# Layer-norm roots of one token block moved from ScalarE to GpSimd, an earlier table load and one matmul tile moved ahead, in a fused attention and gMLP kernel

## The chip, the cores and the metric

The kernel runs on one core of a Trainium2 chip. The metric is the device time of one execution in microseconds (us). Times inside an execution are microseconds from the start of the profiled span. The engines are named as in the profile: PE is TensorE (PEld its weight loads), DVE is VectorE, ACT is ScalarE, POOL is GpSimd, SP is SyncE, whose queue issues nearly all DMAs.

## The reference

The input x has 2048 tokens of 512 channels. It is layer-normalized without weights, and two branches are added to it.

```
xn  = layernorm(x)                        # (x - mean) / sqrt(var + 1e-5)
# branch A: 32 heads of 16, each token attends to 8 tokens: t, t-2, ..., t-14
q, k, v = split(xn @ wqkv)
o   = softmax(mask(q . k[t - 2w]) / 4) applied to v[t - 2w]
A   = o @ wo
# branch B: gMLP, hidden size 688
z   = gelu_tanh(xn @ w_in);  z1, z2 = halves of z
z2  = layernorm(z2)
g   = w_sp @ z2 + b_sp                    # over the 2048 tokens
B   = (z1 * g) @ w_out
out = x + A + B
```

## The kernel before

The 2048 tokens are 16 tiles of 128. Tile i = 4*tb + j belongs to block j (0 to 3); a block so holds the four tiles (tb = 0 to 3) that lie 512 tokens apart. The program is one fixed order of instructions for each engine, written out by hand (no scheduler moves anything): first straight code for the four x blocks, then a string `ORDER` of tokens, each of which issues one step.

**The straight code.** Per tile: `ln_stats` (two DVE instructions, mean and variance into `mv`), `ln_root` (one ACT instruction, `rstd = 1/sqrt(var + eps)`), `ln_apply` (one DVE instruction, x normalized in place), and a transpose into `xnT`, by PE and a copy for the first tiles and by `tr_dma`, a DMA transpose from SP's queue, for the last two tiles of block 1 (`i1`) and all of blocks 2 and 3 (`i2`, `i3`). Between them PE runs q and k of blocks 0 and 1: `qk_part` issues matmuls for two of the four channel chunks of q or k, into a tile `pq` of the main PSUM pool `ps_mm` (three buffers) or `pa3` of the auxiliary pool `ps_aux` (two buffers of one bank), and `qk_copy` is the ACT copy to SBUF. A buffer can be written again only when its copy is done. In block 1 the last of these steps, (1, 3) for tiles 2 and 3, takes a fourth `pq` tile, and the one `ln_root` for all four tiles of block 3 stands on ACT just before its copy; the four applies and DMA transposes of block 3 follow.

**ORDER.** The tokens that matter here: `zJ.T` is a z2 tile, eight matmuls of 344 columns into a `ps_mm` buffer for tile T of block J (L257); `zgJ.T` its gelu on ACT (L275), which frees the buffer; `zsJ.T` a sum of squares on ACT (L281); `qJ.M` and `qcJ.M` are eight matmuls of 512 columns of q or k of block J, which need all four tiles of the block (L315), and their ACT copy (L331); `pG.C` is a DVE product of q and shifted k (L355); `aG` and `bG` are DVE sums over its chunks (L364, L367); `LG` the logits matmuls of group G (L375), which read what `bG` leaves; `X` are the z1 tiles; `wN` loads a tile of w_sp through SP's queue. The order starts

```
z1.3 z2.0 p1.1 z2.2 zg1.3 p0.1 zg2.0 q2.2 zg2.2 p0.3 zs2.2 q2.3 p1.2 qc2.2 p1.3 q2.1 qc2.3 p1.0 z1.0 p0.2
```

Gelu needs another function table on ACT than the roots; the load (L275, ACT_TABLE_LOAD) stands in front of the first gelu, zg1.3.

GpSimd builds a few constants at the start, casts the bias `b` to `b_col` once its DMA has landed (L684), and clears a halo (L697).

Of the kernel before, what the change touches and what calls it, by code (L numbers as in the profile page):

```python
# [8 lines left out]
F32 = mybir.dt.float32  # L9
ACT = mybir.ActivationFunctionType  # L10
ALU = mybir.AluOpType
# [3 lines left out]
P = 128  # L15
# [23 lines left out]
ORD = [1, 2, 3, 0]  # L39
CHUNKS = (1, 1, 1, 1, 1, 1, 1, 1)  # L40
ORDER = """
z1.3 z2.0 p1.1 z2.2 zg1.3 p0.1 zg2.0 q2.2 zg2.2 p0.3 zs2.2 q2.3 p1.2 qc2.2 p1.3 q2.1 qc2.3 p1.0 z1.0 p0.2
qc2.1 w3 z2.1 p0.0 zg1.0 zs1.0 q2.0 p2.2 zg2.1 a1 z2.3 qc2.0 w2 z1.2 zg2.3 p2.3 halo zs2.0 z3.0 p2.0 zg1.2
z1.1 w0 zg3.0 b1 z0.1 zg1.1 p2.1 zs2.3 X0 a0 zg0.1 z3.2 Xg0 zs1.1 z3.3 a2 zg3.2 z3.1 zs1.2 zg3.3 z0.2 b0 zg3.1
X4 b2 zg0.2 zs3.3 L0 L1 Xg4 q3.1 p3.2 zs3.1 p3.0 Lc0 q3.0 Lc1 p3.1 qc3.1 q3.2 p3.3 qc3.0 zs0.1 a3 z0.3 qc3.2
q3.3 zg0.3 p4.1 zs1.3 p4.0 z0.0 qc3.3 X1 p4.2 zg0.0 zs0.3 X2 p4.3 Xg1 X5 st.0 zs2.1 st.1 a4 Xg2 L2 V6 zs0.2
zs3.2 b3 Xg5 V2 b4 Vc6 zs0.0 p5.3 L3 V5 zs3.0 p5.2 Vc2 V1 st.2 p5.1 Vc5 p5.0 V0 st.3 a5 w4 Lc2 Vc1 V4 st.4 Vc0
w1 N1.1 V3 N2.0 Vc4 N1.0 b5 Lc3 V7 N0.0 Vc3 M0.0 N1.2 M0.1 L5 N0.2 L4 Vc7 N3.3 X6 N0.1 M0.2 N0.3 late X3 N3.1
N1.3 N2.1 G0.0 N2.2 Xg6 N2.3 N3.2 N3.0 G0.1 p7.1 G0.2 M0.3 G0.3 p7.2 G4 p6.0 Gi0 w6 Lc4 p6.3 Xg3 p6.2 E0 p7.3
G3 p6.1 U0 S0.0 p7.0 a6 w9 G1 Gi3 Gi4 S0.1 b6 a7 G2 Gi1 w7 U1 S0.2 b7 S0.3 w5 S0.4 Lc5 R0 L6 L7 G6 Lc6 A0 Gi2  # L50
Lc7 U2 U4 mask T4 U3 M1.0 A1 T2 G7 A2 Gi6 w8 A3 wo1.2 A4 T0 A5 X7 M1.1 Gi7 A6 wo1.3 xr0 G5 A7 Xg7 A8 w10 M1.2
# [13 lines left out]
def slot_w(s):  # L65
    return 4 * (s // 4) + 3 - s % 4
# [3 lines left out]
def kernel(  # L70
# [14 lines left out]
    A = nc.scalar  # L85
    G = nc.gpsimd
# [7 lines left out]
    sb = ctx.enter_context(tc.tile_pool(name="sb", bufs=1))  # L94
    work = ctx.enter_context(tc.tile_pool(name="work", bufs=3))
    ps_mm = ctx.enter_context(tc.tile_pool(name="ps_mm", bufs=3, space=PSUM))
    ps_aux = ctx.enter_context(tc.tile_pool(name="ps_aux", bufs=2, space=PSUM))
# [41 lines left out]
    z2 = sb.tile([P, NT, FH], BF16, name="z2")  # L139
# [11 lines left out]
    mv = sb.tile([P, NT, 2], F32, name="mv")  # L151
    rstd = sb.tile([P, NT], F32, name="rstd")
# [4 lines left out]
    zvar = sb.tile([P, NT], F32, name="zvar")  # L157
    zrstd = sb.tile([P, NT], F32, name="zrstd")
    eps_t = sb.tile([P, 1], F32, name="eps_t")


    k_casts = [[] for _ in range(4)]
# [30 lines left out]
                    base=0, pattern=[[-1, P]], channel_multiplier=1)  # L193
    V.memset(ks[:, :, 0:HALO], 0.0)
    V.memset(z1u[:, 0:NZ1 - 1, FH:FPAD], 0.0)
    G.memset(rsel[:], 1.0)
    G.affine_select(out=rsel[:], in_=rsel[:], compare_op=ALU.is_ge, fill=0.0,
                    base=0, pattern=[[-4, 32]], channel_multiplier=1)
# [8 lines left out]
    def ln_stats(i, parts=1):  # L207
        j, tb = i % 4, i // 4
        w = D // parts
        for h in range(parts):  # L210
            V.bn_stats(stats[:, i, 6 * h:6 * h + 6], xall[:, j, tb, w * h:w * h + w])  # L211
        ln_agg(i, parts)
# [4 lines left out]
    def ln_agg(i, parts=1):  # L217
        V.bn_aggr(mv[:, i, :], stats[:, i, 0:6 * parts])  # L218

    def ln_root(sl):  # L220
        A.activation(rstd[:, sl], mv[:, sl, 1], ACT.Abs_reciprocal_sqrt, bias=eps_t[:])

    def ln_apply(i):
        j, tb = i % 4, i // 4
        V.tensor_scalar(xall[:, j, tb, :], xall[:, j, tb, :], mv[:, i, 0:1], rstd[:, i:i + 1],  # L225
                        ALU.subtract, ALU.mult)
# [22 lines left out]
    def tr_dma(i):  # L249
        j, tb = i % 4, i // 4  # L250
        SP.dma_start_transpose(xnT[:, :, i * P:(i + 1) * P], xall[:, j, tb, :])
# [10 lines left out]
    table = [None]  # L262
# [20 lines left out]
    def z2_var():  # L283
        return [lambda: V.tensor_scalar(zmean[:], zsum[:], 1.0 / FH, None, ALU.mult),
                lambda: V.tensor_tensor(zm2[:], zmean[:], zmean[:], ALU.mult),
                lambda: V.scalar_tensor_tensor(zvar[:], zsq[:], 1.0 / FH, zm2[:], ALU.mult, ALU.subtract)]
# [22 lines left out]
    def qk_part(pq, j, m, b0, b1, ccs=(0, 1), p0=None, kcs=range(C)):  # L309
        sd, c0 = m // 2, 2 * (m % 2)  # L310
        p0 = b0 if p0 is None else p0
        xv = xnT[:].rearrange("p k (b j t) -> p k b j t", b=TB, j=4)
        for cc in ccs:
            for kc in kcs:
                PE.matmul(pq[:, cc, p0 * P:(p0 + b1 - b0) * P], wqk[:, sd, kc, c0 + cc:D:C],  # L315
                          xv[:, kc, b0:b1, j, :], start=(kc == 0), stop=(kc == C - 1))
# [7 lines left out]
    def qk_copy(pq, j, m, b0=0, b1=TB, p0=None):  # L324
        sd, c0 = m // 2, 2 * (m % 2)
        p0 = b0 if p0 is None else p0
        if sd == 0:
            dst = qs[:, j, c0:c0 + 2, b0 * P:b1 * P].rearrange("p c (b t) -> p c b t", b=b1 - b0)
        else:
            dst = ks[:, c0:c0 + 2, HALO:HALO + S].rearrange("p c (b j t) -> p c b j t", b=TB, j=4)[:, :, b0:b1, j, :]  # L330
        cast = A.copy(dst, pq[:, :, p0 * P:(p0 + b1 - b0) * P].rearrange("p c (b t) -> p c b t", b=b1 - b0))  # L331
        if sd == 1:
            for i in k_reads[j]:
                tc.declare_no_dep(cast.ins, i, reason="other token columns of the same rows")
            k_casts[j].append(cast.ins)

    def qk_tile():
        return ps_mm.tile([P, 2, TBS], F32, name="pq", tag="mm")
# [8 lines left out]
    def prod_c(g, c):  # L347

        o, h = g // 2, g % 2
        j = ORD[o]  # L350
        q3 = qs[:, j, c, :].rearrange("p (b t) -> p b t", b=TB)
        off = HALO - DIL * slot_w(4 * h)
        k3 = ks[:, c, off:off + S].rearrange("p (b j t) -> p b j t", b=TB, j=4)[:, :, j, :]
        k4 = bass.AP(k3.tensor, k3.offset, [list(x) for x in k3.ap[0:2]] + [[DIL, 4], list(k3.ap[2])])
        prod = V.tensor_tensor(pr[g % 3][:, c].rearrange("p w b t -> p b w t"),  # L355
                        q3.unsqueeze(2).broadcast_to([P, TB, 4, P]), k4, ALU.mult)
        for jj in range(4):
            if jj not in (j, (j - 1) % 4):
                for i in k_casts[jj]:
                    tc.declare_no_dep(prod.ins, i, reason="other token columns of the same rows")  # L360
                k_reads[jj].append(prod.ins)
# [213 lines left out]
    def blk(j):  # L575
        return [4 * tb + j for tb in range(TB)]
# [4 lines left out]
    def blk_cols(j):  # L581
        return slice(j, NT, 4)
# [7 lines left out]
    i2, i3 = blk(2), blk(3)  # L590
    warm_up(10)
    for n in range(2):
        ln_stats(t0[n], 2)
        ln_root(col(t0[n]))
# [7 lines left out]
    pqs = [qk_tile() for _ in range(3)]  # L602
    ln_stats(t0[2])
    ln_root(col(t0[2]))
    tr_copy(t0[1], pts[1], 2, 4)
    q_tile(0, (0, 1))
# [6 lines left out]
    pt2 = tr2(t0[2])  # L613
    q_tile(1, (2, 3))
    ln_root(col(t0[3]))
    tr_copy2(t0[2], pt2)
    ln_apply(t0[3])
# [38 lines left out]
        ln_stats(i2[n])  # L656
    ln_root(slice(2, 7, 4))
    ln_root(slice(10, 15, 4))
    for i in i2:
        ln_apply(i)  # L660
        tr_dma(i)
    for n in range(4):
        ln_stats(i3[n])
    pqs = [qk_tile() for _ in range(3)]
    for c in range(3):
        qk_part(pqs[c], 1, c, 0, 2)
    pa3 = ps_aux.tile([P, 2, 2 * P], F32, name="pa3", tag="aux")
    qk_part(pa3, 1, 3, 0, 2)
    qk_copy(pa3, 1, 3, 0, 2)
    for c in range(3):  # L670
        qk_part(pqs[c], 1, c, 2, 4)
        qk_copy(pqs[c], 1, c)
    pqs[0] = qk_tile()
    qk_part(pqs[0], 1, 3, 2, 4)
    ln_root(blk_cols(3))
    qk_copy(pqs[0], 1, 3, 2, 4)
    for i in i3:
        ln_apply(i)
        tr_dma(i)
    SP.dma_start(r_w[:, 4096:6144].rearrange("p (k f) -> p k f", k=C),  # L680
                 A_wqkv[:, 2 * D:3 * D].rearrange("(k p) f -> p k f", p=P))
    SP.dma_start(w_z1[:], B_w_in[:, 0:FH].rearrange("(k p) f -> p k f", p=P))
# [17 lines left out]
    st = z2_var() + [z2_log, z2_exp]  # L700
# [8 lines left out]
    for tok in ORDER.split():  # L709
        name = tok.rstrip("0123456789.")  # L710
# [31 lines left out]
```

## Time and profile before

| | |
|---|---|
| median of 4 runs | 202.19 us (202.16 to 202.43) |
| profiled execution | 202.3 us, span 200.6 us |
| PE busy | 196.1 us, 98% of the span |
| DVE busy | 184.6 us, 92% |
| ACT busy | 104.0 us, 52% |
| POOL busy | 17.8 us, 9% |
| PE clock granted | 1.00 |

A line of a timeline or group gives, in this order, the start, the length, the engine, the line of the kernel, the operation, output and inputs by their names in the program, the shapes and the count; in square brackets stands how long the engine had been idle before, and what ended that. Instructions of one engine overlap a little (a DVE instruction's successor starts some 0.08 us before its end), and matmuls overlap a lot, so pitches are taken from starts.

### The profile page before, as it was taken

The numbers are of one execution on the slowest core, as the hardware profiler recorded it, in microseconds if no ns is written. First come the engines' busy times: TensorE is split into PE (matmuls) and PEld (weight loads), VectorE is DVE, ScalarE is ACT, GpSimd is POOL, SyncE is SP. The second block draws the span as 40 slices with busy tenths as digits, with TensorE's granted clock in tenths as the row PEclk, the third lists the DMA queues.
The fourth block names the chain that finished last, engine by engine and source line by source line (L and its number), as shares of the span: only waits on it lengthen the run. The fifth ranks groups of instructions, "written<-read, shape, count | busy, mean of one in ns | idle before, by whom it ended". The sixth has DMA issues, their size and how long they took to land.

```text
span 200.6 us, 4090 instructions
## 1 busy us (share of the span) xinstructions
PE 196.1 (98%) x1687; PEld 124.5 (62%) x1691; DVE 184.6 (92%) x249; ACT 104.0 (52%) x176; POOL 17.8 (9%) x14
## 2 busy tenths in 40 slices
PE   7999999999999999999999999999999999999994
PEld 2869745665566666666656666666544646664562
DVE  5689999999989999999979999999999999999624
ACT  3586997899899986363431523808402230331400
POOL 3000000699500000000000000000000000000000
PEclk9999999999999999999999999999999999999999
DMA  5976547960000095534377998199930296219863
GB/s 163 264 240 155 108 82 229 239 120 3 0 0 3 3 165 88 161 82 105 49 164 157 243 227 182 33 231 168 209 80 0 76 215 165 72 34 124 215 209 105
DMA packets 66562, 25.91 MB, mean 129 GB/s; under 512 B 56496, under 2 KB 66288, under 8 KB 66288
## 3 DMA queue, kind: packets, MB, share of 16 engines
q1 hardware_dynamic: 65824, 25.18, 56.7%
q10 hardware_dynamic: 720, 0.48, 0.8%
q8 instruction: 13, 0.21, 0.5%
q14 instruction: 5, 0.04, 0.1%
HBM read 10.13 MB, written 2.10 MB: 61 GB/s over the span
## 4 chain that ended last, share of the span: by engine, by line
PE 90%; DVE 5%; ACT 3%; issue 1%
PE pg L464 37%; PE pz L257 17%; PE pq L315 7%; PE pv L425 7%; PE po L517 6%; PE po L547 6%; DVE stats L211 3%; PE pwm L586 2%; PE pa L547 2%; PE pq L321 1%; ACT r_qk L331 1%; PE pl L375 1%; DVE r_x L225 1%; DVE mv L218 1%; PE po L526 1%; PE pb L517 1%
## 5 line engine op out<-in xcount | busy, mean ns | idle before, releaser
L464 PE MATMUL pg<-z,r_qk 128*128 128x344 bf16 x448 | 66.8, 309 | 0.0
L464 PEld LDWEIGHTS <-r_qk 128*128 128x128 bf16 x448 | 43.8, 98 | 22.0 <-issue 0.4
L439 DVE TENSOR_TENSOR r_pr<-r_x,r_w 128x2048 bf16<-128x2048 bf16 x32 | 38.4, 1219 | 1.3 <-PE pl L375 1.0
L257 PE MATMUL pz<-w_z,xnT 128*128 128x344 bf16 x256 | 39.3, 309 | 0.0
L443 DVE TENSOR_TENSOR r_pr<-r_pr 128x2048 bf16<-128x2048 bf16 x28 | 33.8, 1217 | 0.4
L257 PEld LDWEIGHTS <-xnT 128*128 128x128 bf16 x256 | 25.0, 98 | 13.2 <-issue 0.4
L470 ACT ACTIVATE gs<-pg,b_col 128x688 bf16<-128x688 f32 x16 | 13.2, 833 | 35.4 <-PE pg L464 26.4
L355 DVE TENSOR_TENSOR r_pr<-r_qk 128x2048 bf16<-128x2048 bf16 x24 | 27.8, 1217 | 0.5 <-ACT r_qk L331 0.5
L315 PE MATMUL pq<-xnT,r_w 128*128 128x512 bf16 (+1 forms) x136 | 24.7, 335 | 0.2 <-ACT z L275 0.2
L315 PEld LDWEIGHTS <-r_w 128*128 128x128 bf16 x144 | 15.8, 114 | 7.9 <-issue 0.8
L684 POOL CAST b_col<-b 128x16 f32<-128x16 bf16 x1 | 15.7, 15738 | 34.2 <-DMA b<-in_B_b_sp_dram 34.2
L530 ACT CAST r_qk<-po 128x512 bf16<-128x512 f32 x10 | 5.5, 588 | 22.7 <-PE po L547 22.7
L331 ACT CAST r_qk<-pq 128x1024 bf16<-128x1024 f32 (+1 forms) x16 | 15.4, 984 | 2.5 <-PE pq L315 2.3
L306 ACT ACTIVATE r_uz<-pz 128x688 bf16<-128x688 f32 x16 | 11.7, 740 | 6.6 <-PE pz L257 6.5
L517 PE MATMUL po<-r_lg,r_pr 32*128 32x512 bf16 x192 | 14.5, 375 | 0.0
L425 PE MATMUL pv<-xnT,r_w 128*32 128x512 bf16 x256 | 14.2, 379 | 0.0
L547 PEld LDWEIGHTS <-r_uz 128*128 128x128 bf16 x85 | 8.0, 98 | 9.5 <-issue 1.1
L364 DVE TENSOR_TENSOR r_pr<-r_pr 128x4096 bf16<-128x4096 bf16 x6 | 13.7, 2284 | 0.0
L547 PE MATMUL po<-r_w,r_uz 128*128 128x512 bf16 x56 | 12.7, 379 | 0.5 <-issue 0.5
L281 ACT ACTIVATE junk<-z 128x688 bf16<-128x688 bf16 x16 | 12.4, 774 | 0.1
L275 ACT ACTIVATE z<-pz 128x688 bf16<-128x688 f32 x16 | 11.8, 740 | 1.2 <-PE pz L257 1.2
L425 PEld LDWEIGHTS <-r_w 128*32 128x32 bf16 x256 | 9.5, 138 | 4.2
(85 smaller groups left out, 196.1 us busy)
## 6 DMA issues: line engine op xcount, KB each, us to landing
r_lg<-in_A_wo_dram SPq DMA_DIRECT2D x8, 256.0 KB, 4.0
r_x<-in_A_x_dram SPq DMA_DIRECT2D x12, 128.0 KB, 2.9
out_dram<-r_qk SPq DMA_DIRECT2D x12, 128.0 KB, 2.1
r_w<-in_A_wqkv_dram SPq DMA_DIRECT2D x8, 128.0 KB, 3.4
r_qk<-in_A_x_dram SPq DMA_DIRECT2D x8, 128.0 KB, 2.2
w_z<-in_B_w_in_dram SPq DMA_DIRECT2D x4, 172.0 KB, 4.2
w_z<-in_B_w_in_dram SPq DMA_DIRECT2D x1, 688.0 KB, 5.4
r_w<-in_B_w_out_dram SPq DMA_DIRECT2D x1, 640.0 KB, 6.5
```

What stands on the lines that cost most here:

```text
L257: PE.matmul(pz[:, hh, 0:FHALF], xnT[:, kc, i * P:(i + 1) * P], wz[:, kc, hh * FHALF:(hh + 1) * FHALF], start=(kc == 0), stop=(kc == C - 1))
L315: PE.matmul(pq[:, cc, p0 * P:(p0 + b1 - b0) * P], wqk[:, sd, kc, c0 + cc:D:C], xv[:, kc, b0:b1, j, :], start=(kc == 0), stop=(kc == C - 1))
L331: cast = A.copy(dst, pq[:, :, p0 * P:(p0 + b1 - b0) * P].rearrange("p c (b t) -> p c b t", b=b1 - b0))
L355: prod = V.tensor_tensor(pr[g % 3][:, c].rearrange("p w b t -> p b w t"), q3.unsqueeze(2).broadcast_to([P, TB, 4, P]), k4, ALU.mult)
L364: V.tensor_tensor(pr[g % 3][:, 0:2], pr[g % 3][:, 0:2], pr[g % 3][:, 2:4], ALU.add)
L425: PE.matmul(pv[32 * tb:32 * tb + 32, dd, :], wv[:, kc, 2 * d2 + dd, :], xnT[:, kc, tb * TBS:(tb + 1) * TBS], start=(kc == 0), stop=(kc == ...
L439: V.tensor_tensor(pw_t[n], vp[:, :, off:off + P], a_sb[:, slot_w(w), ts].unsqueeze(1).broadcast_to([P, DH, P]), ALU.mult)
L443: V.tensor_tensor(pw_t[n] if dst is None else dst, pw_t[n], pw_t[m], ALU.add)
L464: PE.matmul(pg[:, hh, 0:FHALF], wsp[n][:, k, :], z2[:, k, hh * FHALF:(hh + 1) * FHALF], start=(k == 0), stop=(k == NT - 1))
L517: PE.matmul(pc, op[32 * tb:32 * tb + 32, d, o * P:(o + 1) * P], wo_r[32 * tb:32 * tb + 32, d, cs], start=(d == 8), stop=False, tile_positi ...
L547: mm = PE.matmul(pc, uT[:, o % 2, m, tb * P:(tb + 1) * P], wout[:, m, cs], start=False, stop=(m == MCH - 3))
L684: G.tensor_copy(b_col[:], b16[:])
```

## The change

Three things are changed in the straight code, with one move in ORDER that goes with them.

1. The roots of block 3 are computed on GpSimd, tile by tile, by two dependent instructions on 128x1 each: variance plus eps, and that to the power of a new constant tile `mhalf` (-0.5). The one ACT root for the four tiles is gone. The stats, applies and DMA transposes of block 3 are interleaved: the first tile is applied ahead of the stats of the last, and the last is applied behind the product p1.1, which leaves ORDER for this place.
2. The gelu table is loaded right behind the roots of block 2 on ACT, ahead of the copies of q and k of block 1.
3. The last q and k step of block 1 takes a second `pa3` tile of the auxiliary PSUM pool, and not a fourth `pq`; in ORDER z1.2 moves from behind q of block 2 to third place, ahead of z2.2 and q2.2, and its gelu zg1.2 with it.

```diff
-z1.3 z2.0 p1.1 z2.2 zg1.3 p0.1 zg2.0 q2.2 zg2.2 p0.3 ...
-... a1 z2.3 qc2.0 w2 z1.2 zg2.3 p2.3 halo zs2.0 z3.0 p2.0 zg1.2
-z1.1 ...
+z1.3 z2.0 z1.2 z2.2 zg1.3 p0.1 zg2.0 zg1.2 q2.2 zg2.2 p0.3 ...
+... a1 z2.3 qc2.0 w2 zg2.3 p2.3 halo zs2.0 z3.0 p2.0 z1.1 ...
...
+    G.memset(mhalf[:], -0.5)
...
+    def ln_root_pool(i):
+        G.tensor_tensor(rstd[:, i:i + 1], mv[:, i, 1:2], eps_t[:], ALU.add)
+        G.tensor_tensor(rstd[:, i:i + 1], rstd[:, i:i + 1], mhalf[:], ALU.pow)
...
     ln_root(slice(10, 15, 4))
+    A.preload_act_table_set("gelu_apprx_tanh_and_others")
+    table[0] = "gelu"
     for i in i2:
         ln_apply(i)
         tr_dma(i)
-    for n in range(4):
+    for n in range(3):
         ln_stats(i3[n])
+        ln_root_pool(i3[n])
+    ln_apply(i3[0])
+    tr_dma(i3[0])
+    ln_stats(i3[3])
+    ln_root_pool(i3[3])
+    for i in i3[1:3]:
+        ln_apply(i)
+        tr_dma(i)
...
-    pqs[0] = qk_tile()
-    qk_part(pqs[0], 1, 3, 2, 4)
-    ln_root(blk_cols(3))
-    qk_copy(pqs[0], 1, 3, 2, 4)
-    for i in i3:
-        ln_apply(i)
-        tr_dma(i)
+    pa3 = ps_aux.tile([P, 2, 2 * P], F32, name="pa3", tag="aux")
+    qk_part(pa3, 1, 3, 2, 4, p0=0)
+    qk_copy(pa3, 1, 3, 2, 4, p0=0)
+    prod_c(1, 1)
+    ln_apply(i3[3])
+    tr_dma(i3[3])
```

More of the change, by code (lines that the diff above doesn't have):

```diff
@@ L41 @@
 ORDER = """
[L42 to L48, printed above, removed]
+z1.3 z2.0 z1.2 z2.2 zg1.3 p0.1 zg2.0 zg1.2 q2.2 zg2.2 p0.3 zs2.2 q2.3 p1.2 qc2.2 p1.3 q2.1 qc2.3 p1.0
+z1.0 p0.2 qc2.1 w3 z2.1 p0.0 zg1.0 zs1.0 q2.0 p2.2 zg2.1 a1 z2.3 qc2.0 w2 zg2.3 p2.3 halo zs2.0 z3.0 p2.0 z1.1
+w0 zg3.0 b1 z0.1 zg1.1 p2.1 zs2.3 X0 a0 zg0.1 z3.2 Xg0 zs1.1 z3.3 a2 zg3.2 z3.1 zs1.2 zg3.3 z0.2 b0 zg3.1 X4
+b2 zg0.2 zs3.3 L0 L1 Xg4 q3.1 p3.2 zs3.1 p3.0 Lc0 q3.0 Lc1 p3.1 qc3.1 q3.2 p3.3 qc3.0 zs0.1 a3 z0.3 qc3.2 q3.3
+zg0.3 p4.1 zs1.3 p4.0 z0.0 qc3.3 X1 p4.2 zg0.0 zs0.3 X2 p4.3 Xg1 X5 st.0 zs2.1 st.1 a4 Xg2 L2 V6 zs0.2 zs3.2
+b3 Xg5 V2 b4 Vc6 zs0.0 p5.3 L3 V5 zs3.0 p5.2 Vc2 V1 st.2 p5.1 Vc5 p5.0 V0 st.3 a5 w4 Lc2 Vc1 V4 st.4 Vc0 w1
+N1.1 V3 N2.0 Vc4 N1.0 b5 Lc3 V7 N0.0 Vc3 M0.0 N1.2 M0.1 L5 N0.2 L4 Vc7 N3.3 X6 N0.1 M0.2 N0.3 late X3 N3.1
 N1.3 N2.1 G0.0 N2.2 Xg6 N2.3 N3.2 N3.0 G0.1 p7.1 G0.2 M0.3 G0.3 p7.2 G4 p6.0 Gi0 w6 Lc4 p6.3 Xg3 p6.2 E0 p7.3
@@ L159 @@
     eps_t = sb.tile([P, 1], F32, name="eps_t")
+    mhalf = sb.tile([P, 1], F32, name="mhalf")
     k_casts = [[] for _ in range(4)]
```

## Prediction

> **What bounds the kernel now.** I read the page's busy shares first, then its chain of waits, then the list of waits of TensorE, and then the timelines of the engines around the one place they point to.
>
> The busy shares and the chain (share of the span by engine):
>
> ```profile
> PE 196.1 (98%) x1687; PEld 124.5 (62%) x1691; DVE 184.6 (92%) x249; ACT 104.0 (52%) x176; POOL 17.8 (9%) x14
> ...
> PE 90%; DVE 5%; ACT 3%; issue 1%
> ```
>
> TensorE works 98% of the span and is 90% of the chain that ends last: only time in which PE stands still, or work taken off PE, can shorten this kernel. The change takes no matmul away. So I ask where PE waits (us in total, times, longest):
>
> ```profile
> PE pwm L586 <- DVE warm L189: 1.1, 1, 1.1
> PE po L547 <- issue: 0.5, 3, 0.2
> PE pq L315 <- ACT z L275: 0.2, 1, 0.2
> ```
>
> The first is the start, the second lies at the output matmuls; the change touches neither. The third is in its reach. The timeline of PE and of ACT there (start, length, instruction):
>
> ```profile
> 18.27 3.66 PE L315 MATMUL pq<-xnT,r_w 128*128 128x256 bf16 x32
> 21.77 3.66 PE L257 MATMUL pz<-w_z,xnT 128*128 128x344 bf16 x24
> 25.59 5.34 PE L315 MATMUL pq<-xnT,r_w 128*128 128x512 bf16 x24 [0.16 <-ACT z L275]
> ...
> 22.82 0.57 ACT L331 CAST r_qk<-pq 128x512 bf16<-128x512 f32 x1
> 23.41 1.28 ACT L275 ACT_TABLE_LOAD   x1
> 24.70 0.74 ACT L275 ACTIVATE z<-pz 128x688 bf16<-128x688 f32 x1
> 25.34 0.20 ACT L275 ACTIVATION_READ_ACCUMULATOR z<-pz 128x1 f32 x1
> ```
>
> Matmul durations overlap, so starts count, not ends. The 88 z matmuls from 34.83 to the first L375 start at 47.75 are 0.146 apart. 24 of them from 21.77 end their issue at 21.77 + 24 x 0.146 = 25.27; the first q matmul of block 2 starts at 25.59. PE lost 0.32 there (the profile calls 0.16 of it idle). It wanted the PSUM buffer of z1.3, the first of the three pz: its gelu waited for the table load behind the root of block 3 and the last copy of q and k (23.41 to 24.70), ran from 24.70 and gave the buffer up after its accumulator read at 25.54. From there to 143 I find no other gap between matmul starts over 0.1 us.
>
> **The change part by part.**
>
> *PE.* No matmul is added or removed. The last eight matmuls of q and k of block 1 go to the auxiliary PSUM pool, so z1.3, z2.0 and z1.2 take the three main buffers and z2.2 the first again. With no stall PE starts z1.3 at 21.77, z2.0 at 22.94, z1.2 at 24.10, z2.2 at 25.27 (8 x 0.146 = 1.17 each) and q2.2 at 26.43. So q2.2, and all up to z2.3, start 26.43 - 25.59 = 0.84 later than now; z1.2, which stood behind z2.3, is then already done, and from z3.0 on everything starts 0.32 earlier.
>
> *ACT.* The load moves behind the roots of block 2, which end at 18.45. It then covers 18.47 to 19.75, where ACT now does the pa copy (18.47, 0.58) and idles 0.29. Pitches as in the trace (0.87 a block copy, 0.55 half a one): pa copy from 19.75, pq copies from 20.25, 21.13, 22.00, second pa copy 22.87 to 23.45. The three buffers are free at about 21.1, 22.0, 22.9, where PE asks at 21.77, 22.94, 24.10: least slack 0.6. Gelu of z1.3 runs from 23.4, its buffer is free at 24.3 and asked for at 25.27; that of z2.0 at 25.1 for 26.43. No wait is left and 0.32 of PE is the gain. The root of block 3 on ACT (128x4, 0.30) goes too, which only helps.
>
> The Trainium skill, page "ScalarE: Activation LUTs", section "What ACT_TABLE_LOAD costs", puts a switch at 1.28 for the load and 1.38 for a drain. In the trace the copy before the load ends at 23.39 and the gelu after it starts at 24.70, so only the 1.28 is there, and I use that. By the page the first pq copy would free its buffer at 22.5 and PE would wait 0.7 for it: a loss of 0.4 in place of the gain.
>
> *DMA.* z2.0 and z2.2 come no earlier than now, q2.2 0.84 later. SyncE issues the eight transposes of blocks 2 and 3 one after another, about 1.3 apart, from 18.69; the fourth (issued 22.70) lands at 25.17 by the trace's landing events, so it would pass for q2.2 even without the extra tile. The fifth to eighth, of block 3, cannot go before 24.01, when the queue is free; their data is normalized by then, or, for the last, well before its slot at 29.18. So the loads queued behind them (value weights, w_z1, bias) keep their times, and z3.0, the first reader of block 3, comes at 36.9.
>
> *DVE and GpSimd.* This is the unknown. The lines of DVE, and of GpSimd, now:
>
> ```profile
> 21.70 0.66 DVE L211 BATCH_NORM_STATS2 stats<-r_x 128x6 f32<-128x512 bf16 x1
> 22.40 0.18 DVE L218 BATCH_NORM_AGGREGATE mv<-stats 128x2 f32<-128x6 f32 x1
> 22.95 1.38 DVE L225 TENSOR_SCALAR r_x<-r_x,mv,rstd 128x512 bf16<-128x512 bf16 x4 [0.37 <-ACT rstd L221]
> 24.25 9.16 DVE L355 TENSOR_TENSOR r_pr<-r_qk 128x2048 bf16<-128x2048 bf16 x8
> ...
> 45.62 1.21 DVE L367 TENSOR_TENSOR r_pr<-r_pr 128x2048 bf16<-128x2048 bf16 x1
> 46.75 1.21 DVE L367 TENSOR_TENSOR r_uz<-r_uz 128x2048 bf16<-128x2048 bf16 x1
> 47.89 4.62 DVE L355 TENSOR_TENSOR r_pr<-r_qk 128x2048 bf16<-128x2048 bf16 x4
> 52.54 2.29 DVE L364 TENSOR_TENSOR r_pr<-r_pr 128x4096 bf16<-128x4096 bf16 x1
> ...
> 1.51 0.21 POOL L197 TENSOR_SCALAR_AFFINE_SELECT rsel<-rsel 128x32 bf16<-128x32 bf16 x1
> 1.79 0.21 POOL L199 TENSOR_SCALAR_AFFINE_SELECT rsel<-rsel 128x32 bf16<-128x32 bf16 x1
> ...
> 36.83 15.74 POOL L684 CAST b_col<-b 128x16 f32<-128x16 bf16 x1 [34.16 <-DMA b<-in_B_b_sp_dram]
> ```
>
> DVE's order becomes stats 0, 1, 2, apply 0, stats 3, apply 1, apply 2, p1.1, apply 3, p0.1. With its pitches (stats and aggregate 0.80, apply 0.32, product 1.14), means are ready at 20.20, 21.00, 21.80 and 22.92, and the applies come up at 21.70, 22.82, 23.14 and 24.60. A root is two dependent GpSimd instructions on 128x1, an add and a power; call the pair R. Nothing shows them. The nearest rows are the two dependent selects: 0.28 from start to start, and 0.21 for the last, so R = 0.5. The far row is the cast: 15.74 for 16 columns. It starts while DVE runs products without a break and ends at 52.57, just after DVE's first gap (52.51 to 52.54): GpSimd stood behind DVE's two-input work. I take 0.5, as the selects read and write SBUF and are small and chained as the pair is; the power may cost several selects, so up to 1.5 is kept in the range. Below 0.5 nothing is gained, since PE does not wait for it.
>
> With R = 0.5 roots 0 to 2 are ready in time if GpSimd gets in beside the stats. Root 3 does not: behind stats 3 DVE runs apply 1, apply 2 and p1.1 without a gap, as before the cast's end, so GpSimd starts when DVE stops for apply 3 at 24.68. Then p0.1 starts at 24.7 + R + 0.32, against 24.25 + 1.14 = 25.39 now: DVE is R - 0.37 later, 0.13 for 0.5. Behind that wait are queued p0.1 and all products and pair sums up to b0, which the logits matmuls of chunk 0 read (L375, PE at 47.75); b0 ends at 46.83 now. PE comes for it at 47.43, so DVE may be 0.6 late at no cost, and 0.9 late before the whole gain is gone. At 0.13 the cost is nothing. The cover is this 0.6.
>
> That GpSimd gets in beside the stats is not shown here. The Trainium skill, page "SBUF — State Buffer", section "Who interferes with whom", says that a VectorE instruction with one SBUF input outside the two-port modes leaves GpSimd alone, which would cover the stats. If the stats blocked it too, roots 0 to 2 would also wait for a DVE gap, DVE would be some three R late, less the 0.37, and the sum about 202.4; the range holds it.
>
> GpSimd's later work is the bias cast, which waits for its DMA until 36.83, and a memset at 52.50; the roots are long done. A memset more at 1.3 lies in idle time.
>
> *Sum.* 0.32 off PE, nothing added: the profiled execution, 202.3 with a span of 200.6, would be 202.0 with 200.3. The median of the runs is 202.19, so 201.87, -0.16%. Differences within 0.2% (0.40) are about what a measurement of this kernel can tell from no change, so the forecast itself lies inside.
>
> **The rivals.**
>
> *GpSimd's root is slow, and DVE becomes the bound of the stretch to 47.75 (slower).* The four roots are serial: root 3 ends no earlier than 20.2 + 4R, and each apply waits. At R = 1.0 DVE is 0.2 to 0.9 late and the gain is whole or gone; at R = 1.5 apply 2 waits until 24.8, p1.1 ends at 26.3, p0.1 starts at 26.6, DVE is 1.2 late, PE waits at L375, net +0.3; at 2.0 DVE is 3.2 late and the time 204.5. It decides from R = 1.2. For it: the only GpSimd instruction beside busy DVE took 15.74. Against: that one could find no gap, and here each DVE wait for a root opens one.
>
> *Another wait takes the stall's place.* PE reaches z2.2 or q2.2 and meets a late ACT copy or a late transpose. For it: ACT is 88% busy from 25.6 to 47.75 (19.57 of 22.15), and the slack of the first buffer is 0.6. Against: every slack worked out above is 0.6 or more. Time 202.0 to 202.4.
>
> *The gain is a little more than 0.32*, with the 0.1 gaps at changes of matmul form, or by the spread of the runs (202.16 to 202.43): 201.7.
>
> **How the numbers follow.** Forecast (stall gone, R under 1): 0.62. It is 0.08 short of the 0.2% bound, less than the runs' spread, so 0.25 of this falls to faster and 0.37 to same. Slow root: 0.25, of which 0.22 slower and 0.03 same. Another wait: 0.10, of which 0.07 same and 0.03 slower. A larger gain by something I do not see 0.02, another loss 0.01. Faster 0.27, same 0.47, slower 0.26. The range: from 201.65 (the forecast less a spread) to 202.9 (R about 1.6, +0.7); it leaves out a root of 1.7 and more, some 0.13, and 0.05 below. Within it the forecast's own range is 201.65 to 202.05.
>
> **What would show it.** Right: PE's list of waits no longer has q behind ACT's z; the table load starts at about 18.5; z2.2 and q2.2 start at 25.27 and 26.43; L375 starts at 47.4. DVE waits for GpSimd once, before apply 3, by some 0.5. Wrong: DVE waits for a GpSimd root in more than one place or by over 1 us, L375 starting after 47.75 behind DVE's b0, or PE waiting for pq copies at 21.8.

## The result, and the profile after

The changed kernel takes 201.73 us (median of 31 runs, 201.36 to 202.13) against 202.08 for the kernel before in the same sessions (51 runs, 201.72 to 202.63). The ratio is 0.9982, with a 95% interval of 0.9976 to 0.9987: 0.18% faster, or 0.36 us. The forecast was 0.16%.

The profiled execution of the changed kernel took 201.59 with a span of 199.9, 0.7 less than before. That is more than the change: the spans have to be split. TensorE's list of waits first (us in total, times, longest):

```profile
PE pwm L592 <- DVE warm L190: 1.0, 1, 1.0
PE po L553 <- issue: 0.5, 3, 0.2
PE pt L238 <- DVE r_x L231: 0.5, 1, 0.5
```

The wait of q for ACT's gelu (L315 behind L275 before) is no longer in it. A wait at the first transposes has come in, which lies at 5 us. It is not the change's: the runs below without the moved tile and with the late load have the same code up to there and do not show it, and the run with the moved tile alone has 0.2 of it. The timeline of PE, with the same stretch as was shown of before:

```profile
17.89 2.78 PE L321 MATMUL pq<-xnT,r_w 128*128 128x256 bf16 x24
20.51 1.04 PE L321 MATMUL pa<-xnT,r_w 128*128 128x256 bf16 x8
21.38 4.83 PE L263 MATMUL pz<-w_z,xnT 128*128 128x344 bf16 x32
26.05 5.34 PE L321 MATMUL pq<-xnT,r_w 128*128 128x512 bf16 x24
...
35.29 11.83 PE L263 MATMUL pz<-w_z,xnT 128*128 128x344 bf16 x80
47.05 0.61 PE L381 MATMUL pl<-r_pr,rsel 128*32 128x512 bf16 x8
```

Four z tiles run without a break from 21.38, and q follows after 32 x 0.146 = 4.67 with no gap. From the start of z1.3 to the first logits matmul it is 47.05 - 21.38 = 25.67, against 47.75 - 21.77 = 25.98 before: 0.31 less, the whole stall. The other 0.39 of the profile's 0.7 is in the start of z1.3 (21.38 against 21.77). I set that aside as spread: in the profiles of the experiments below, except the one that delays the start itself, z1.3 starts anywhere from 21.21 to 21.89. I therefore compare the length from z1.3 to the first logits matmul, called the stretch from here on, and the timed ratios, and not the spans.

ACT in the changed kernel:

```profile
17.77 0.30 ACT L223 ACTIVATE rstd<-mv,eps_t 128x2 f32<-128x2 f32 x1 [1.29 <-DVE mv L220]
18.08 1.28 ACT L665 ACT_TABLE_LOAD   x1
19.38 0.59 ACT L337 CAST r_qk<-pa 128x512 bf16<-128x512 f32 x1
19.86 2.85 ACT L337 CAST r_qk<-pq 128x1024 bf16<-128x1024 f32 x3
22.57 0.63 ACT L337 CAST r_qk<-pa 128x512 bf16<-128x512 f32 x1
23.05 0.80 ACT L281 ACTIVATE z<-pz 128x688 bf16<-128x688 f32 x1
```

The load ends at 19.36 and the copy behind it starts at 19.38: 1.28 and nothing more, as before. The first gelu starts at 23.05, 1.67 behind z1.3; before it was 24.70 - 21.77 = 2.93.

DVE and GpSimd around the roots:

```profile
22.44 0.70 DVE L231 TENSOR_SCALAR r_x<-r_x,mv,rstd 128x512 bf16<-128x512 bf16 x2
23.06 1.22 DVE L361 TENSOR_TENSOR r_pr<-r_qk 128x2048 bf16<-128x2048 bf16 x1
24.72 0.41 DVE L231 TENSOR_SCALAR r_x<-r_x,mv,rstd 128x512 bf16<-128x512 bf16 x1 [0.44 <-POOL rstd L227]
25.05 8.03 DVE L361 TENSOR_TENSOR r_pr<-r_qk 128x2048 bf16<-128x2048 bf16 x7
...
19.90 0.19 POOL L226 TENSOR_TENSOR rstd<-mv,eps_t 128x1 f32<-128x1 f32 x1 [17.20 <-DVE mv L220]
20.17 0.55 POOL L227 TENSOR_TENSOR rstd<-rstd,mhalf 128x1 f32<-128x1 f32 x1
22.60 0.27 POOL L226 TENSOR_TENSOR rstd<-mv,eps_t 128x1 f32<-128x1 f32 x1 [0.22 <-DVE mv L220]
22.95 1.74 POOL L227 TENSOR_TENSOR rstd<-rstd,mhalf 128x1 f32<-128x1 f32 x1
```

The first root takes 0.82 (19.90 to 20.72), the add 0.27 of it to the next start and the power 0.55. DVE waits for GpSimd once, by 0.44, where the prediction had put it. p0.1 starts at 25.05, 3.67 behind z1.3, against 25.39 - 21.77 = 3.62 before: DVE is 0.05 late.

### The profile page after: what moved, and what is told of

Read it like the earlier page. It is cut to its first block, busy times and chain, and to the rows that moved or that the text cites. A ratio compares the mean times of both kernels' runs of the same rounds, so it can differ in the third digit from the quotient of the medians.

```text
span 199.9 us, 4098 instructions
## 1 busy us (share of the span) xinstructions
PE 195.0 (98%) x1687; PEld 123.8 (62%) x1691; DVE 184.5 (92%) x249; ACT 103.9 (52%) x175; POOL 22.3 (11%) x23
## 2 busy tenths in 40 slices
DMA packets 66562, 25.91 MB, mean 130 GB/s; under 512 B 56496, under 2 KB 66288, under 8 KB 66288
## 4 chain that ended last, share of the span: by engine, by line
PE 95%; DVE 2%; DMA 1%; issue 0%; ACT 0%
PE pg L470 37%; PE pz L263 19%; PE pq L321 11%; PE pv L431 7%; PE po L523 6%; PE po L553 6%; PE pa L553 2%; PE pq L327 2%; DMA r_x<-in_A_x_dram 1%; PE pl L381 1%; PE pa L321 1%; PE po L532 1%; DVE stats L213 1%; PE pb L523 1%; PE pt L238 0%
## 5 line engine op out<-in xcount | busy, mean ns | idle before, releaser
L321 PE MATMUL pq<-xnT,r_w 128*128 128x512 bf16 (+1 forms) x128 | 23.8, 339 | 0.0
L337 ACT CAST r_qk<-pq 128x1024 bf16<-128x1024 f32 x15 | 14.9, 1015 | 2.4 <-PE pq L321 2.3
```

## The experiments

Two theories stood at the start. The first is the prediction's: PE had waited for one gelu that stood behind root, copy and table load on ACT; that wait is gone, and DVE has some slack for the slower roots. The second gives the gain to the extra tile, as time for the transposes of block 2.

**The moved tile alone.** The kernel before, with only the order and the PSUM pool changed; root and table load stay on ACT where they were.

```diff
-z1.3 z2.0 p1.1 z2.2 zg1.3 ...
+z1.3 z2.0 p1.1 z1.2 z2.2 zg1.3 ...    (zg1.2 moved too)
-    pqs[0] = qk_tile()
-    qk_part(pqs[0], 1, 3, 2, 4)
+    pa3 = ps_aux.tile([P, 2, 2 * P], F32, name="pa3", tag="aux")
+    qk_part(pa3, 1, 3, 2, 4, p0=0)
```

> The kernel before, with only the extra z2 tile ahead of q of block 2 and the second pa3 tile; root of block 3 on ScalarE and late table load stay, p1.1 stays in ORDER. Theory (the gain is the wait of PE for the gelu of z1.3, which stands behind root, copy and table load): z2.2 now asks for that buffer, at the same 25.27, and it is free at 25.5, so the stall only moves from q2.2 to z2.2, some 0.3 us; time as before, ratio 1.000 (0.999 to 1.001). Rival (the gain comes from the tile that gives the transposes of block 2 more time): ratio 0.998, no gap at z2.2.

Measured: 1.0003 (0.9994 to 1.0012), no gain. PE's timeline in that run:

```profile
21.59 3.66 PE L257 MATMUL pz<-w_z,xnT 128*128 128x344 bf16 x24
25.42 1.33 PE L257 MATMUL pz<-w_z,xnT 128*128 128x344 bf16 x8 [0.16 <-ACT z L275]
```

The stall stands at z2.2 now, as long as before: 25.42 where 21.59 + 24 x 0.146 = 25.09 was due. Stretch 25.99. The extra tile does not remove the wait for the gelu; this fits the first theory.

**Without the moved tile.** The changed kernel, with z1.2 and zg1.2 back behind q of block 2.

```diff
-z1.3 z2.0 z1.2 z2.2 zg1.3 p0.1 zg2.0 zg1.2 q2.2 ...
+z1.3 z2.0 z2.2 zg1.3 p0.1 zg2.0 q2.2 ...
```

> The changed kernel without the extra tile: z1.2 stays behind q of block 2, so q2.2 is the fourth step after the copies. Theory as predicted (the fourth transpose of block 2 lands before q2.2 asks, 25.17 against 25.27): full gain, ratio 0.998. Rival, from the trace of the changed kernel (that transpose took 3.3 us from its issue and landed at 25.48, where q2.2 without the tile would ask at 24.88): PE waits up to 0.6 us for the DMA and the gain is gone, ratio 0.999 to 1.001, with a gap before q2.2.

Measured: 1.0034 (1.0022 to 1.0045), slower than the kernel before, which none of the expectations went as far as. PE:

```profile
21.79 3.66 PE L263 MATMUL pz<-w_z,xnT 128*128 128x344 bf16 x24
26.05 5.34 PE L321 MATMUL pq<-xnT,r_w 128*128 128x512 bf16 x24 [0.59 <-DMA xnT<-r_x]
```

The wait for ACT is gone, and a longer one for the fourth transpose of block 2 has taken its place: q2.2 starts 0.76 later than the matmuls before it allow. The stretch is 26.43, 0.45 above before and 0.76 above the changed kernel; the timed ratio has 0.69 and 1.05 (+0.0052). The profiled run took 202.76, as the median of its runs (202.77), so it did not wait less than the others; where the remaining 0.24 to 0.29 lie is open.

So each half alone gains nothing or loses. The question was why this transpose is late. In the kernel before and in the run with the moved tile alone its 16 parts all land about 2.5 after the issue (25.17 for 22.70, 24.89 for 22.42). In every profile with the roots on GpSimd and no extra instruction on VectorE, one part lands 0.8 to 0.9 behind the other 15 (here 25.91 and 25.12); in one of them, the run with copies on ScalarE below, two parts do. One thing in the DMA view of this window (23.5 to 26) is not there in the kernel before, where it ran at 20.55: an 8 KB transfer of instructions (q14 in the list). There it ran beside the first transpose of block 2, which landed 3.5 after its issue (18.69 to 22.20), against 2.5 in the changed kernel (18.31 to 20.80); q waits for the last of the four, so that cost nothing. The DMA view of the run without the moved tile, 23.5 to 26 (packets, MB, share of the 16 DMA engines):

```profile
q1 hardware_dynamic: 1085, 0.26, 51.6%
q14 instruction: 1, 0.01, 1.3%
```

**Moving the instruction transfer.** The run without the moved tile, with eight small extra instructions at the very start, on VectorE, ScalarE or GpSimd, meant to shift the point at which that engine's code is fetched.

```diff
+    for n in range(8):
+        V.memset(spare[:, n:n + 1], 0.0)       # or G.memset, or A.copy from eps_t
```

> The run without the extra tile (no_move, ratio 1.0034), with eight more small memsets on VectorE at the start, in idle time. There one of the 16 parts of the fourth transpose of block 2 landed 0.8 late, and an 8 KB instruction transfer ran beside it, at 24.5. Theory (that transfer delays the part, and where it falls depends on how many instructions an engine has before it): if these eight move it out of 23.5 to 25.5, the transpose lands 2.5 after its issue, PE's wait before q2.2 falls from 0.6 to 0.1 or less, and the ratio is 0.998; if they do not move it (it belongs to another engine), all stays as in no_move, 1.003. Rival (the part is late because of the changed order of VectorE, GpSimd or the DMA queue): the part is late wherever the transfer falls, 1.003.

> As the run with eight memsets on VectorE, but with eight small copies on ScalarE at the start. Theory: if the transfer moves out of 23.5 to 25.5, the transpose lands 2.5 after its issue and the ratio is 0.998, else 1.003. Rival: the part is late wherever the transfer falls, 1.003.

> As the run with eight memsets on VectorE, but with eight memsets on GpSimd at the start. Theory: if the transfer moves out of 23.5 to 25.5, the transpose lands 2.5 after its issue and the ratio is 0.998, else 1.003. Rival: the part is late wherever the transfer falls, 1.003.

Measured: on VectorE 0.9987 (0.9978 to 0.9996), on GpSimd 1.0021 (1.0013 to 1.0030), on ScalarE 1.0143 (1.0120 to 1.0166). With the memsets on VectorE the transfer runs at 17.7, and the DMA view of the window 23.5 to 26 has no instruction queue:

```profile
q1 hardware_dynamic: 1033, 0.25, 49.8%
```

All 16 parts of the transpose land by 25.38 for an issue at 22.90, and PE:

```profile
21.87 3.66 PE L266 MATMUL pz<-w_z,xnT 128*128 128x344 bf16 x24
25.51 5.34 PE L324 MATMUL pq<-xnT,r_w 128*128 128x512 bf16 x24
```

The gap before q2.2 is 0.14 instead of 0.76, stretch 25.81. On GpSimd the transfer stays (23.9, 2.7 behind z1.3, as without the memsets), one part lands 0.8 late and the gap is 0.74. So the transfer is VectorE's instructions, and it is the cause of the late part: eight memsets that do no work of the kernel save 0.34% against eight on GpSimd, timed in the same session, and 0.47% against the same kernel without them. Why the change itself had moved the transfer from 20.55 to 24.06 is not shown. The time of the run on ScalarE tells nothing: its copies pulled in a second table load at the start, and z1.3 came at 22.84. Its profile fits, though. Two 8 KB transfers of instructions fall on the transpose there, at 25.48 and 25.54 (without the copies one runs at 24.48 and the other only at 35.1), and two parts landed late (26.88 and 26.96, the other 14 by 26.14). What made its other runs 1.2 to 1.5 slower than the profiled one is open.

**The table load at its old place.** The changed kernel without the early load; it then comes in front of the first gelu.

```diff
-    A.preload_act_table_set("gelu_apprx_tanh_and_others")
-    table[0] = "gelu"
```

> The changed kernel without the early load: the table is loaded in front of the gelu of z1.3, right behind the last copy. Theory (with the root gone from ScalarE and z1.2 ahead, z2.2 asks for the buffer of z1.3 at 25.27 on the clock of the trace before, and gelu from 23.95 gives it free at 24.8): no stall, ratio 0.998 as the changed kernel. Rival (the place of the load is what makes the gain): a gap of 0.2 to 0.4 before z2.2, ratio 0.999 to 1.000.

Measured: 0.9981 (0.9972 to 0.9990), stretch 25.67, no gap: the same as the changed kernel. ACT:

```profile
21.99 0.62 ACT L337 CAST r_qk<-pa 128x512 bf16<-128x512 f32 x1
22.62 1.28 ACT L281 ACT_TABLE_LOAD   x1
23.92 0.74 ACT L281 ACTIVATE z<-pz 128x688 bf16<-128x688 f32 x1
```

The gelu starts 2.23 behind z1.3 (21.69). With the root on ACT it was 2.93 in the kernel before. The copies go through without the root and the wait for DVE in front of it, and the buffer is free by 24.8, where z2.2 asks at 21.69 + 24 x 0.146 = 25.19. Moving the load added nothing; taking the root off ACT was enough, with the moved tile. The reverse, an early load with the root still on ACT, was not run: the root needs the other table.

**Without the product in front of the last apply.**

```diff
-    prod_c(1, 1)
     ln_apply(i3[3])
     tr_dma(i3[3])
+    prod_c(1, 1)
```

> The changed kernel with p1.1 behind the last apply and not ahead of it. Theory (GpSimd stands while VectorE runs a two-input product): the power of root 3 takes about 0.55 as the other three do, and not 1.74; VectorE waits for it about 0.7 and p1.1 and p0.1 follow; p0.1 starts within 0.2 us of where it starts now, time the same, ratio 0.998. Rival (the fourth power is slow for another reason): it takes 1.7 again, VectorE stops for 1.8, p0.1 comes 1.2 later and PE waits at the first logits matmul for 0.6: ratio 1.001.

Measured: 0.9989 (0.9980 to 0.9998), an interval that overlaps the changed kernel's; stretch 25.66. GpSimd's fourth root and DVE's wait:

```profile
22.91 0.27 POOL L226 TENSOR_TENSOR rstd<-mv,eps_t 128x1 f32<-128x1 f32 x1 [0.22 <-DVE mv L220]
23.25 0.60 POOL L227 TENSOR_TENSOR rstd<-rstd,mhalf 128x1 f32<-128x1 f32 x1
...
23.89 0.41 DVE L231 TENSOR_SCALAR r_x<-r_x,mv,rstd 128x512 bf16<-128x512 bf16 x1 [0.44 <-POOL rstd L227]
```

The power takes 0.60 here and 1.74 with the product beside it. DVE waits 0.44 either way. The product hides none of the root: while it runs the power stands, and what it was to cover is waited for afterwards.

**A slower root.** The changed kernel with one, and with three, more power instructions (into a spare tile) ahead of the last one of root 3.

```diff
         G.tensor_tensor(rstd[:, i:i + 1], mv[:, i, 1:2], eps_t[:], ALU.add)
+        for _ in range(extra):                  # root 3 only: 1 or 3
+            G.tensor_tensor(spare[:], rstd[:, i:i + 1], mhalf[:], ALU.pow)
```

> The changed kernel with one more power instruction, into a spare tile, ahead of the power of root 3, so that this root ends about 0.6 us later. Theory (VectorE may be 0.6 late at the first logits matmul before PE waits; it is 0.05 late now, by the trace 0.55 of slack): VectorE's wait grows from 0.44 to about 1.0, the cost is 0 to 0.15, ratio 0.998 to 0.999. Rival (VectorE's lateness goes through in full): ratio 1.001.

> As the run with one more power, with three: root 3 ends about 1.7 us later. Theory: VectorE is 1.75 late at its sums b0, 0.6 of it is covered, PE waits about 1.1 before the first logits matmul and the time is 1.1 above the changed kernel, ratio 1.003 to 1.004. Rival 1 (in full): 1.7 above, ratio 1.0065. Rival 2 (VectorE's lateness is not felt at all, PE has other work): ratio 0.998.

Measured: one more 0.9988 (0.9978 to 0.9999), three more 1.0052 (1.0038 to 1.0066). DVE's waits for the root, with one and with three:

```profile
25.86 0.41 DVE L234 TENSOR_SCALAR r_x<-r_x,mv,rstd 128x512 bf16<-128x512 bf16 x1 [1.07 <-POOL rstd L230]
```

```profile
26.84 0.41 DVE L234 TENSOR_SCALAR r_x<-r_x,mv,rstd 128x512 bf16<-128x512 bf16 x1 [2.32 <-POOL rstd L230]
```

The wait is 0.63 and 1.88 above the changed kernel's 0.44. The stretch is 25.80 and 27.05, so 0.13 and 1.38 above 25.67. In both, 0.50 is swallowed and the rest goes through at the first logits matmul, with three as a wait for DVE's sum:

```profile
48.67 0.61 PE L384 MATMUL pl<-r_pr,rsel 128*32 128x512 bf16 x8 [1.31 <-DVE r_pr L376]
```
The timed difference of the second, 1.0052 - 0.9982 = 0.0070 or 1.41 us, is that 1.38.

## Why the prediction was right, and where it was not

- *The stall.* 0.32 was to go and 0.31 went; the ratio's interval, 0.05% to either side, holds the forecast. The cause was the right one: the moved tile alone only carried the wait from q2.2 to z2.2.
- *ACT.* The new timeline came as worked out (first gelu 1.67 behind z1.3, worked out as 1.6). But I gave the gain to the moved load, and the root's going was enough: with the load late the time is the same. The load's price of 1.28 held; the drain of the Trainium skill's page "ScalarE: Activation LUTs", section "What ACT_TABLE_LOAD costs", is not to be seen in either place of the load: 0.02 lies between its end and the next instruction in both.
- *The moved tile.* "It would pass for q2.2 even without the extra tile" is the step that failed. I took the landing of the fourth transpose (25.17) from the trace before as fixed. In the changed kernel it lands at 25.48 in a profile that starts 0.39 earlier, as VectorE's instruction transfer now falls on it; q2.2 asks at 26.05, 0.57 later, so the tile covers it. Without the tile the change would have been a loss of 0.34%: the rival "another wait takes the stall's place" was at work, hidden by a part of the change that I had called unneeded, and its price was larger than the 202.0 to 202.4 I gave it (202.77). That the whole came out as forecast is in this point luck. Even with the transfer out of the way the margin of 0.1 was not there: the transpose landed at 25.38 and q2.2 asked at 21.87 + 24 x 0.146 = 25.37.
- *The root's price.* The term R was put at 0.5 from two selects and measures 0.82: the add is like a select (0.27 to the next start, 0.28 there), the power is two of them (0.55). GpSimd did get in beside the stats, as the Trainium skill's page "SBUF — State Buffer", section "Who interferes with whom", has it: the powers of roots 0 to 2 take 0.55 to 0.56 beside them.
- *Root 3.* I had the whole pair wait for DVE to stop. Only the power did; the add ran beside the apply in 0.27 instead of 0.19. This error and that in R cancel by luck: p0.1 was to be 0.13 late and is 0.05 late; with R at 0.82 my rule would have made it 0.45.
- *The slack of DVE.* 0.6 was predicted; 0.05 used and 0.50 left make 0.55, and beyond it lateness goes through one to one. The rival of the slow root was rightly built, and rightly did not occur.

## What to carry to other kernels

When an engine that sets the time waits for a short chain on another one, list all that stands ahead on that engine and ask which piece must go: here the small root, which itself waited for a third engine, and not the table load beside it. A landing time read from one trace is not a constant under a change of program; a step that looks unneeded by a margin of 0.1 us deserves a run of its own. Here a small power on GpSimd could not be hidden behind a two-input product of VectorE: with the product ahead of the wait or behind it, VectorE waited 0.44 and the stretch was the same.

## What the runs showed of the hardware that was not expected

An 8 KB transfer of VectorE's instructions delayed the kernel's own DMA beside it. Where it fell on the fourth transpose of block 2, one of the 16 parts landed 0.8 us late (25.91 where the other 15 had landed by 25.12), and q2.2 started 0.76 late. Eight 128x1 memsets on VectorE at the start moved the transfer from 24.5 to 17.7 and the gap before q2.2 fell to 0.14, with 0.47% of the time. The kernel before has the pattern too, where nothing waits for it: a 16 KB transfer of instructions starts at 27.32, and of the transpose issued at 25.31 fifteen parts land by 27.74 and one at 29.75.

A power on 128x1 takes GpSimd 0.55 beside stats and 1.74 when a product of VectorE starts 0.12 after it; it then ends 0.4 after the product (24.68 and 24.28).
